# One visit fewer to the 64-column tiling: kv of two batches and two remainder tiles together, and the last q loaded early

## The chip, the cores and the metric

The kernel runs on one core of one Trainium2 chip. The metric is the device time of one execution in microseconds. Ratios are the mean time of one kernel's fast runs over the mean of the other's fast runs of the same rounds, so they are not quite the ratios of the medians that stand beside them.

## The reference, cut to what matters

```python
kv  = einsum('bhsd,bhse->bhde', k, v)              # 8 batches, 8 heads, 576 rows, head size 64
out = einsum('bhsd,bhde->bhse', q, kv)
x   = out / sqrt(mean(out*out, -1) + 1e-6) * g_norm  # then heads side by side: (8, 576, 512)
xn  = (x - mean) / sqrt(var + 1e-6) * g_ln
y   = x + relu(xn @ w_ch1) @ w_ch2                 # 512 -> 2048 -> 512
```

The two products of the last line are nearly all of the TensorE work. A batch has 576 rows, which is four tiles of 128 and a remainder of 64. The remainders of two batches share one tile ("remainder tile 5" holds those of batches 4 and 5, "remainder tile 7" those of 6 and 7), and the four remainder tiles make up a ninth block at the end.

## The kernel before

Everything is written as one stream per engine, in an order that an agenda of slots sets by hand. A slot is four 128x512 matmuls; block b has 32 slots from 32b, 16 for the first product and 16 for the second. What an agenda entry emits stands in each engine's queue at that place. It fixes the order, not the time.

```python
def kv_of(*bs):                      # k^T v per head: 64-column matmuls, then four casts for two batches
    kv_ps = ps_m.tile([128, len(bs), HP, D], f32, tag="misc", name="kv_ps")
    for i, b in enumerate(bs):
        ...                          # 40 matmuls per batch
    for i, b in enumerate(bs):
        kvp = held[b] = kv_pack[b % 4]
        nc.scalar.copy(kvp[:D, :, :D], kv_ps[:D, i])
        nc.scalar.copy(kvp[D:, :, D:], kv_ps[D:, i])

def turn_q_dma(b):                   # q copied to another order by VectorE, transposed by DMA
    ...
    nc.vector.tensor_copy(q_p.rearrange("p j h d -> p h j d"), q_in[b % NB])
    nc.sync.dma_start_transpose(...)

def rem_tile(b):                     # stationary of 64 columns: again the 64-column tiling
    mms = []
    for half, bb in enumerate((b - 1, b)):
        qt, kp = qts.pop(bb), held.pop(bb)
        mms.append((slice(half * 64, (half + 1) * 64), lambda hp, qt=qt: qt[:, J, hp, :64], kp))
    ...

# plan_tile(s, make, turn_at, on_pe, x_at): matmuls and square and reduce at slot s; root,
# reciprocal, y, x, xc at x_at (s + 2 if not given); the deviation 4 later; the transpose at turn_at

at(132, lambda: load_batches((("q", 6), ("k", 6), ("v", 6), ("k", 7), ("v", 7)), turned_q(5)))
at(164, lambda: load_batches((("q", 7),), turned_q(6)))
for s, bs, rem, x_at, tn in (..., (152, (6, 7), 5, 154, 160)):
    at(s, lambda bs=bs: kv_of(*bs))
    plan_tile(s + .1, lambda rem=rem: rem_tile(rem), tn, False, x_at)
plan_tile(210, lambda: rem_tile(7), 216, False)
```

So kv of batches 6 and 7, with remainder tile 5, is one visit to the array's 64-column tiling in the second product of block 4, and remainder tile 7 is another in the second product of block 6.

## Time and profile before

| | before |
|---|---|
| median of the first three runs | 288.96 us (288.9 to 289.06) |
| TensorE busy, share of the span | 97% |
| longest wait of TensorE after 20 us | none worth naming |
| starts of consecutive 128x512 matmuls | 0.216 us apart |

TensorE is the bound (97% busy, and 91% of the chain that ended last): what counts is the sum of its matmuls and anything that makes its queue stand. I cut the stretch of the change at the first matmul of each product, which the timeline gives. Below is the view of busy time by stretch: block 4's second product, block 5's first, block 5's second with block 6's first, and block 6's second. The columns are the stretch, its length, then busy time and instructions of TensorE, its weight loads, VectorE, ScalarE and GpSimd, the granted clock, the DMA share and the GB/s.

```profile
154.71:170.46 15.75, 15.64 (x155) 7.90 (x156) 9.55 (x21) 5.68 (x15) 1.53 (x3) 1.00 0.99 144
170.46:184.95 14.49, 14.38 (x78) 6.95 (x78) 9.83 (x22) 12.54 (x27) 0.00 (x0) 1.00 0.48 96
184.95:213.47 28.52, 28.36 (x143) 13.43 (x145) 16.27 (x35) 15.03 (x34) 0.00 (x0) 1.00 0.39 79
213.47:227.73 14.26, 14.21 (x71) 6.43 (x72) 8.60 (x19) 4.11 (x11) 0.00 (x0) 1.00 0.37 79
```

A product alone is 64 x 0.216 = 13.8 us. The first row has 1.9 us more, which is the visit of kv and remainder 5 and tile 0 of batch 6; the last has 0.44 more, which is the visit of remainder 7: 0.22 for its eight matmuls and 0.22 for entering and leaving the 64-column tiling, of which entering is 0.09 (214.98 to 215.29, where 0.216 is usual). Note in the second row that ScalarE (the fourth busy time) works 12.5 us of 14.5: the first product is where ScalarE has least room. Together the four stretches take 73.02 us.

### The profile page before, as it was taken

The numbers are of one execution on the slowest core, as the hardware profiler recorded it, in microseconds if no ns is written. First come the engines' busy times: TensorE is split into PE (matmuls) and PEld (weight loads), VectorE is DVE, ScalarE is ACT, GpSimd is POOL, SyncE is SP. The second block draws the span as 40 slices with busy tenths as digits, with TensorE's granted clock in tenths as the row PEclk, the third lists the DMA queues.
The fourth block names the chain that finished last, engine by engine and source line by source line (L and its number), as shares of the span: only waits on it lengthen the run. The fifth ranks groups of instructions, "written<-read, shape, count | busy, mean of one in ns | idle before, by whom it ended". The sixth has DMA issues, their size and how long they took to land.

```text
span 286.7 us, 5727 instructions
## 1 busy us (share of the span) xinstructions
PE 277.8 (97%) x2269; PEld 158.0 (55%) x2295; DVE 150.0 (52%) x331; ACT 152.9 (53%) x333; POOL 43.1 (15%) x73
## 2 busy tenths in 40 slices
PE   7889999999999999999999999999999999999995
PEld 3579755995579654454444544444444444444444
DVE  5774119937997883774376475763679200220022
ACT  3477844995468643971387338911893066016500
POOL 8522510041036005000710020000000000000000
PEclk9999999999999999999999999999999999999999
DMA  7999999969997979986999995047203410230033
GB/s 215 198 209 202 201 191 197 214 111 188 144 180 124 185 141 172 214 101 127 159 215 190 120 160 135 18 82 158 56 18 72 95 37 0 48 81 19 0 73 76
DMA packets 67419, 36.76 MB, mean 128 GB/s; under 512 B 35517, under 2 KB 62525, under 8 KB 67393
## 3 DMA queue, kind: packets, MB, share of 16 engines
q0 software_dynamic: 28720, 18.29, 44.2%
q1 hardware_dynamic: 38160, 17.39, 30.4%
q10 hardware_dynamic: 512, 0.72, 0.8%
q8 instruction: 18, 0.29, 0.5%
q14 instruction: 9, 0.07, 0.1%
HBM read 36.71 MB, written 9.44 MB: 161 GB/s over the span
## 4 chain that ended last, share of the span: by engine, by line
PE 91%; DMA 2%; DVE 2%; ACT 2%; issue 1%; DVEq 0%; POOLq 0%
PE p L432 43%; PE p L416 42%; PE o_ps L274 3%; DMA v_in<-in_v_dram 2%; PE kv_ps L247 2%; ACT m L419 1%; DVE x_blk L292 0%; DVE xc L552 0%; ACT xT_blk L353 0%; PE tp L351 0%; ACT rms L311 0%; PE odd L226 0%; DVE ss L518 0%; PE tp L559 0%; DVE ss L301 0%
## 5 line engine op out<-in xcount | busy, mean ns | idle before, releaser
L416 PE MATMUL p<-xT_blk,w_sb 128*128 128x128 bf16 (+2 forms) x1015 | 131.2, 285 | 0.9
L432 PE MATMUL p<-w_sb,m 128*128 128x512 bf16 (+2 forms) x592 | 126.2, 368 | 1.2 <-issue 0.5
L419 ACT ACTIVATE m<-p 128x512 bf16<-128x512 f32 x144 | 85.2, 596 | 46.7 <-PE p L416 44.3
L416 PEld LDWEIGHTS <-w_sb 128*128 128x128 bf16 x1024 | 78.6, 98 | 44.5 <-issue 1.1
L432 PEld LDWEIGHTS <-m 128*128 128x128 bf16 x608 | 57.3, 98 | 62.9
L437 DVE SCALAR_TENSOR_TENSOR o_sb<-p,rstd,x_blk 128x512 f32<-128x512 f32 (+2 forms) x38 | 27.2, 721 | 47.7 <-PE p L432 42.1
L280 ACT ACTIVATE sq<-o_ps 128x512 f32<-128x512 f32 x35 | 20.9, 596 | 26.7 <-PE o_ps L274 26.5
L343 ACT ACTIVATE dev<-x_blk,st_blk 128x512 f32<-128x512 f32 x36 | 25.7, 714 | 13.1 <-DVE st_blk L329 13.1
L301 DVE TENSOR_REDUCE ss<-sq 128x8 f32<-128x512 f32 x35 | 23.7, 678 | 17.0 <-ACT sq L280 17.0
L335 DVE SCALAR_TENSOR_TENSOR xc<-x_blk,st_blk,g_ln_sb 128x512 bf16<-128x512 f32 x34 | 25.6, 752 | 1.2
L306 DVE TENSOR_TENSOR y<-o_ps,inv 128x512 f32<-128x512 f32 x33 | 22.8, 692 | 3.1
L325 DVE SCALAR_TENSOR_TENSOR x_blk<-y,g_norm_sb 128x512 f32<-128x512 f32 x33 | 22.8, 692 | 1.1
L318 DVE RECIPROCAL inv<-rms 128x8 f32<-128x8 f32 x36 | 7.3, 202 | 23.3 <-ACT rms L311 23.3
L425 DVE RECIPROCAL rstd<-rstd 128x4 f32<-128x4 f32 x9 | 1.6, 175 | 29.9 <-ACT rstd L424 29.8
L311 ACT ACTIVATE rms<-ss,eps_sb 128x8 f32<-128x8 f32 x36 | 10.6, 295 | 11.5 <-DVE ss L301 11.3
L274 PEld LDWEIGHTS <-qt 128*128 128x128 bf16 (+1 forms) x156 | 10.3, 100 | 6.0 <-issue 0.4
L274 PE MATMUL o_ps<-kv_pack,qt 128*128 128x128 bf16 (+1 forms) x156 | 13.6, 220 | 0.0
L98 POOL COPY gate<-qt 1x1 bf16<-1x1 bf16 x5 | 0.9, 177 | 82.4 <-DMA qt<-q_p 82.4
L199 PE MATMUL p<-fill_sb 128*128 128x512 bf16 x26 | 7.8, 452 | 1.3 <-DVE eps_sb L138 1.2
L252 ACT CAST kv_pack<-kv_ps 64x256 bf16<-64x256 f32 x7 | 2.6, 366 | 10.7 <-PE kv_ps L247 10.7
L343 ACT ACTIVATION_READ_ACCUMULATOR dev<-x_blk,st_blk 128x1 f32 x36 | 6.8, 190 | 0.0
L247 PEld LDWEIGHTS <-k_in 128*64 128x64 bf16 x280 | 4.9, 112 | 2.4 <-issue 2.3
(82 smaller groups left out, 112.6 us busy)
## 6 DMA issues: line engine op xcount, KB each, us to landing
out_dram<-o_sb SPq DMA_DIRECT2D x66, 128.0 KB, 2.6
w_sb<-in_moe_w_ch_dram POOLq DMA_DIRECT2D x8, 512.0 KB, 15.2
q_in<-in_q_dram POOLq DMA_DIRECT2D x7, 320.0 KB, 9.7
k_in<-in_k_dram POOLq DMA_DIRECT2D x7, 320.0 KB, 8.7
v_in<-in_v_dram POOLq DMA_DIRECT2D x7, 320.0 KB, 10.3
q_in<-in_q_dram POOLq DMA_DIRECT2D x8, 256.0 KB, 10.5
k_in<-in_k_dram POOLq DMA_DIRECT2D x7, 256.0 KB, 9.3
v_in<-in_v_dram POOLq DMA_DIRECT2D x7, 256.0 KB, 12.3
```

Of the source, the lines that this page charges most:

```text
L247: nc.tensor.matmul(kv_ps[hh * D:hh * D + D, i, hp, :], lhsT=k_in[b % NB][:, h, j, :], rhs=v_in[b % NB][:, h, j, :], start=(j == 0), stop=( ...
L274: nc.tensor.matmul(flat[rows, hp * 128:(hp + 1) * 128], lhsT=lhsT_of(hp), rhs=kvp[:, hp, :], start=True, stop=True)
L280: nc.scalar.activation(self.sq_t, self.o_ps, func=AF.Square)
L301: nc.vector.tensor_reduce(self.ss, self.sq_t, axis=AX.X, op=ALU.add)
L306: nc.vector.tensor_mul(self.y_t, self.o_ps, self.inv().to_broadcast([128, H, D]))
L325: nc.vector.scalar_tensor_tensor(x_blk[:, ts].rearrange("p (h d) -> p h d", h=H), in0=self.y_t, scalar=1.0, in1=g_norm_sb.to_broadcast([12 ...
L335: nc.vector.scalar_tensor_tensor(self.xc_t, in0=x_blk[:, self.ts], scalar=st[:, 1, self.ts:self.ts + 1], in1=g_ln_sb, op0=ALU.add, op1=ALU ...
L343: nc.scalar.activation(dev, x_blk[:, ts], func=AF.Square, bias=st[:, 1, ts:ts + 1], accum_out=st[:, 2, ts:ts + 1])
L416: nc.tensor.matmul(p1[:, i, :], lhsT=w1_sb[:, kk, de * 128:(de + 1) * 128], rhs=blk[2][:, kk, sl], start=(kk == 0), stop=(kk == nK - 1))
L419: nc.scalar.activation(m1[:, de0:de0 + per, sl], p1, func=AF.Relu)
L432: nc.tensor.matmul(p2[:, c0:c1], lhsT=m1s[b][:, de, ts * 128:(ts + 1) * 128], rhs=w2_sb[:, de, c0:c1], start=(de == 0), stop=(de == nDe - 1))
L437: nc.vector.scalar_tensor_tensor(o_sb[:, c0:c1], in0=p2[:, c0:c1], scalar=rstds[b][:, ts:ts + 1], in1=blks[b][0][:, ts, c0:c1], op0=ALU.mu ...
```

## The change

Its intent: enter and leave the 64-column tiling once instead of twice. For that remainder 7 must stand beside kv of 6 and 7, so q of batch 7 is loaded and turned (transposed) beside that of 6, the visit moves nine slots later with kv of 7 before that of 6, and the tiles of batch 6 move too.

```diff
-            qt, kp = qts.pop(bb), held.pop(bb)
+            qt, kp = qts[bb], held[bb]
+            if b < B - 1:
+                del qts[bb], held[bb]
...
-    at(132, lambda: load_batches((("q", 6), ("k", 6), ("v", 6), ("k", 7), ("v", 7)),
+    at(132, lambda: load_batches((("q", 6), ("q", 7), ("k", 6), ("v", 6), ("k", 7), ("v", 7)),
                                  turned_q(5)))
-    at(164, lambda: load_batches((("q", 7),), turned_q(6)))
...
-                                 (152, (6, 7), 5, 154, 160)):
+                                 (161, (7, 6), 5, 162, 168)):
...
-    plan_tile(210, lambda: rem_tile(7), 216, False)
+    plan_tile(161.2, lambda: rem_tile(7), 170, False, 164)
...
-                                *((b, 32 * b - 43.3, 32 * b - 32, 5) for b in range(5, B))):
+                                (5, 116.7, 128, 5), (6, 147, 165, 4.5), (7, 151, 192, 5)):
```

## The prediction

> **What bounds the kernel now.** I read the page first: busy shares, then the chain that ended last.
>
> ```profile
> PE 277.8 (97%) x2269; PEld 158.0 (55%) x2295; DVE 150.0 (52%) x331; ACT 152.9 (53%) x333; POOL 43.1 (15%) x73
> ...
> PEclk9999999999999999999999999999999999999999
> ...
> PE 91%; DMA 2%; DVE 2%; ACT 2%; issue 1%; DVEq 0%; POOLq 0%
> ```
>
> The end is set by TensorE's own queue, at full clock. The view of TensorE's waits, asked over the whole span, has no wait after the first 20 us worth a microsecond:
>
> ```profile
> PE even L226 <- DMA v_in<-in_v_dram: 1.4, 1, 1.4
> PE p L199 <- DVE eps_sb L138: 1.2, 1, 1.2
> PE p L432 <- issue: 0.5, 3, 0.2
> PE tp L559 <- DVE xc L552: 0.4, 1, 0.4
> ```
>
> From 60 us on TensorE runs matmul after matmul; the starts of 128x512 matmuls lie 0.216 us apart (three starts in a row just before the late remainder visit: 214.55, 214.76, 214.98). So the program is a sum of matmuls, and a change counts only if it removes TensorE time or makes TensorE wait. A slot of the agenda is four such matmuls, 4 x 0.216 = 0.864 us; a block has 32 slots, 16 for its first product (L416) and 16 for its second (L432).
>
> The timeline of TensorE and of ScalarE around the visits that move shows both sides of this change (columns: start us, us, engine, line, operation, tiles, count, idle before and releaser):
>
> ```profile
> 161.71 1.46 PE L247 MATMUL kv_ps<-v_in,k_in 128*64 128x64 bf16 x80
> 163.00 0.39 PE L274 MATMUL o_ps<-kv_pack,qt 128*64 128x128 bf16 x8
> 163.32 7.08 PE L432 MATMUL p<-w_sb,m 128*128 128x512 bf16 x31
> 170.24 0.39 PE L274 MATMUL o_ps<-kv_pack,qt 128*128 128x128 bf16 x4
> ```
>
> ```profile
> 163.21 0.37 ACT L252 CAST kv_pack<-kv_ps 64x256 bf16<-64x256 f32 x1 [3.95 <-PE kv_ps L247]
> 163.58 0.37 ACT L253 CAST kv_pack<-kv_ps 64x256 bf16<-64x256 f32 x1
> 163.97 0.37 ACT L252 CAST kv_pack<-kv_ps 64x256 bf16<-64x256 f32 x1
> 164.35 0.37 ACT L253 CAST kv_pack<-kv_ps 64x256 bf16<-64x256 f32 x1
> 164.75 0.60 ACT L280 ACTIVATE sq<-o_ps 128x512 f32<-128x512 f32 x1
> ```
>
> Here kv of 6 and 7 (80 small matmuls) is followed at once by remainder tile 5 (8 matmuls), whose kv was cast long ago; the four casts of the fresh kv run while TensorE is back at large matmuls. The late visit, remainder 7 alone, stands in the middle of block 6's second product:
>
> ```profile
> 214.55 0.81 PE L432 MATMUL p<-w_sb,m 128*128 128x512 bf16 x3
> 215.29 0.41 PE L274 MATMUL o_ps<-kv_pack,qt 128*64 128x128 bf16 x8
> 215.63 1.04 PE L432 MATMUL p<-w_sb,m 128*128 128x512 bf16 x4
> ```
>
> [...]the last large matmul before the late visit started at 214.98, the first tile matmul at 215.29, 0.309 us later where the usual distance is 0.216, so entering costs 0.09. [...]in this trace the one 1.38 us wait of TensorE (before 8.20 us) left the granted clock at full. [...]both batches' kv share one 128x512 f32 tile, and here the first cast started at 163.21, after all 80 kv matmuls had been issued (the eight after them started at 163.00).
>
> **The change part by part.**
>
> 1. *One visit fewer.* The late visit: from the large matmul at 214.98 to the next at 215.63 is 0.656 us, less the 0.216 that one large matmul takes anyway: 0.44. Its four pairs in steady run are 0.052 to 0.056 apart, about 0.22 us, and those are still paid in the merged visit. Saved: 0.44 - 0.22 = **0.22 us**. The visit of kv and remainder 5 moves from block 4's second product (slot 152) to slot 161, block 5's first product; its own cost (161.40 to 163.32, less 0.216: 1.71 us) is the same in either place.
>
> 2. *A new wait for the casts.* In the built order of the changed kernel the eight matmuls of remainder 7 come straight after the eight of remainder 5, and the first waits for ScalarE: it reads kv of 6 and 7, which the 80 matmuls just before have made. Order (7, 6) puts 6's casts last, and the first matmul reads 6's. On the distances of the old trace: kv starts at t; remainder 5 at t+1.29; remainder 7 could start at t+1.51; first cast at t+1.50, fourth ends at t+3.01 (161.71 to 164.72), plus 0.05 for the signal: t+3.06. TensorE idles about **1.55 us**. [...]
>
> 3. *ScalarE and VectorE in block 5's first product.* The old trace of this stretch, 170.4 to 184.3:
>
> ```profile
> 170.40:184.30 13.90, 13.79 (x77) 6.71 (x75) 9.27 (x20) 11.88 (x26) 0.00 (x0) 1.00 0.50 101
> ```
>
> ScalarE (fourth pair of numbers) is busy 11.88 of 13.90, because each slot needs one 0.60 us relu. The change puts in four casts (1.5), two squares (1.2), two roots (0.6) and two deviations (1.8): about 5 us, and takes out about 0.9 (tile 3 of batch 6 moves to slot 178). 11.9 + 5.1 - 0.9 = 16.1 against 13.9 + 1.55 of stall + the visit of 1.7 = 17.2: it fits, barely. VectorE gets the two remainder tiles at 0.69 (reduce) + 2.6 (reciprocal, y, x, xc) = 3.3 us each, ahead of tile 0 of batch 6, in order. I walked the three queues by hand with the trace's durations, from slot 160 at 168.7 (170.4 less the 1.71 now still to come): casts end 172.66; relu of slot 161 at 173.96; VectorE finishes remainder 5's xc at 177.4 and 7's at 180.0; only then tile (6,0)'s reduce, 180.04 to 180.73. ScalarE stands at that tile's root until 180.76, with the relu of slot 167 behind it. TensorE has three buffers for this product, so slot 170 must wait for that relu: 181.60 in place of 181.28 (0.32), then 0.33 and 0.12 in the next two slots, after which it runs level. Sum **0.77 us**, the least certain term: a lag 0.7 us less erases it, 0.7 more doubles it.
>
> 4. *Loads and turns.* Two loads less late, none less in all; one 1x1 gate copy drops. Batch 7's q takes its 3.5 us of traffic ahead of k and v, so the last v lands near 163 instead of 159.60. kv now starts near 169.6: hidden. q of 7 turned: VectorE copies it near 160.6 to 161.4, SyncE issues its transpose behind that of batch 5's last tile, near 165.6, and with the 5.9 us of batch 6's (161.05 to 166.91) it lands near 171.5, just before the casts end at 172.66. Hidden by 1.2 us. Batch 5's last transposed tile landed at 167.35; its product now starts at 168.7 instead of 170.4. Hidden by about 1.3.
>
> Sum: 288.96 - 0.22 + 1.55 + 0.77 = 291.06. I shade the third term a little and say **290.8**.
>
> **The rivals.** (a) *The saving alone*: the 0.22 us shows, 288.7. It needs the casts to be done when remainder 7 starts; the old trace says they end 1.5 us after that[...]. Against it. (b) *Only the cast wait*, with the third term absorbed: 288.96 - 0.22 + 1.55 = 290.3. For it: TensorE's own stall gives ScalarE 1.5 us to catch up. (c) *A transfer becomes the wait*: more traffic up to 163 us beside the transposes of q could delay batch 5's last transposed tile past 168.7, or q of 7 past 172.7. A microsecond or two late means 291.5 to 292.5. Against: both margins are over 1 us and the loads end well before. (d) *ScalarE becomes the bound of the whole first product*: 16.1 against 17.2 us says no, but if remainder tiles lag, more than three slots stall: 292. (e) The clock drops after the idle time: 1.55 us is close to the harmless 1.38 seen, so no.
>
> **Range and chances.** Range 289.7 to 292.0: below (b) by 0.6 if the casts start sooner than I think, above the sum by 0.9 if (c) or (d) joins in. Two per cent is 5.8 us either way. Faster by that is impossible from a visit worth 0.44 us in all; slower needs over twice the stall that I find. Chances: faster 0.01, same 0.97, slower 0.02.
>
> **What the new profile would show.** Step 1: no 128*64 matmuls in block 6's second product; one run of 80 and 16 in block 5's first. Step 2: a wait of remainder 7's first matmul for the kv casts of about 1.5 us, the largest late wait in TensorE's view. Step 3: small waits of the L416-line matmuls for relus near 181 to 184, the root of tile (6,0) waiting for its reduce. Step 4: no wait for a transfer. I am wrong if the first idle is near zero (the wait asks for less than the last cast), if the turned q and not a cast ends it, or if the loss is spread over many slots.

That no other matmul runs while one waits, on which step 2 rests, was the assumption; the changed kernel's trace shows it. The 3.5 us of traffic in step 4 is the estimate: the two loads of a q move 320 and 256 KB (the page), which at the 186 GB/s of the trace before from 140 to 164 us takes 3.2 us. Measured, the last v landed 4.5 us later (164.11 for 159.60).

## The result, and the profile after

The changed kernel took 291.81 us in the median of four runs (291.51 to 292.11), the kernel before 288.93 in the same rounds: ratio 1.0102, 95% interval 1.0085 to 1.0120. It is about 1% slower. The profiled runs lie 292.11 against 288.75, so the two traces differ by 3.4 us, somewhat more than the medians' 2.9: the profiled run of the changed kernel is the slowest of its four.

The view of TensorE's waits over the whole span of the changed kernel, the three rows of it that are new (what waited, for what; us in total, times, longest):

```profile
PE o_ps L274 <- ACT kv_pack L253: 1.4, 1, 1.4
...
PE o_ps L274 <- DMA qt<-q_p: 0.9, 1, 0.9
...
PE p L418 <- ACT m L421: 0.5, 2, 0.3
```

The rows left out are those of the start and of the issue, as before. Remainder 7 (L274) waits for a cast, then for a transpose of q, and the first product (L418) waits twice for relus. The same three on TensorE's timeline:

```profile
169.56 1.46 PE L247 MATMUL kv_ps<-v_in,k_in 128*64 128x64 bf16 x80
170.85 0.39 PE L274 MATMUL o_ps<-kv_pack,qt 128*64 128x128 bf16 x8
172.61 0.22 PE L274 MATMUL o_ps<-kv_pack,qt 128*64 128x128 bf16 x1 [1.37 <-ACT kv_pack L253]
173.71 0.41 PE L274 MATMUL o_ps<-kv_pack,qt 128*64 128x128 bf16 x7 [0.88 <-DMA qt<-q_p]
...
182.73 1.02 PE L418 MATMUL p<-xT_blk,w_sb 128*128 128x512 bf16 x4 [0.29 <-ACT m L421]
183.92 2.86 PE L418 MATMUL p<-xT_blk,w_sb 128*128 128x512 bf16 x11 [0.16 <-ACT m L421]
```

The eight matmuls of remainder 5 go through at once. The first of remainder 7 (batch 6's half) starts when the last cast is done, at 172.61; the second (batch 7's half) needs q of 7, which is not turned until 173.7. From 170.85 to 174.28 no matmul of the first product runs, though its last transposed tile had landed at 168.28: what stands behind a waiting matmul here waited with it. Around 182 to 184 the product stands twice more. The timeline of VectorE and of ScalarE says why; the rows are remainder 7's xc, the reduce of tile (6,0) behind it, and the root that waits for that reduce with a relu behind it:

```profile
180.51 0.75 DVE L335 SCALAR_TENSOR_TENSOR xc<-x_blk,st_blk,g_ln_sb 128x512 bf16<-128x512 f32 x1
181.18 0.68 DVE L301 TENSOR_REDUCE ss<-sq 128x8 f32<-128x512 f32 x1
```

```profile
181.90 0.30 ACT L311 ACTIVATE rms<-ss,eps_sb 128x8 f32<-128x8 f32 x1 [1.31 <-DVE ss L301]
182.10 0.58 ACT L421 ACTIVATE m<-p 128x512 bf16<-128x512 f32 x1
```

Busy time by stretch, cut at the same four products:

```profile
154.79:168.60 13.81, 13.76 (x64) 6.23 (x64) 7.17 (x14) 2.50 (x7) 0.00 (x0) 1.00 1.21 184
168.60:188.56 19.96, 17.05 (x171) 8.66 (x172) 12.83 (x29) 14.96 (x35) 0.00 (x0) 1.00 0.45 92
188.56:217.31 28.75, 28.59 (x147) 13.63 (x149) 18.48 (x41) 16.63 (x38) 0.00 (x0) 1.00 0.28 60
217.31:231.12 13.81, 13.76 (x64) 6.27 (x64) 5.69 (x12) 2.50 (x7) 0.00 (x0) 1.00 0.36 77
```

The four stretches take 76.33 us, 3.31 more than before. The last row shows what the change was made for: 13.81 in place of 14.26, so the late visit's 0.45 us is gone. The second row shows the price: in 19.96 us TensorE is busy 17.05. Outside these stretches the two traces run alike: 0.08 us of difference before them, at 154.7, and the rest of the end's 3.4 us lies within.

### The profile page after: what moved, and what is told of

Same layout as the page of the kernel before. It is cut to its first block, busy times and chain, and to the rows that moved or that the text cites. A ratio compares the mean times of both kernels' runs of the same rounds, so it can differ in the third digit from the quotient of the medians.

```text
span 290.1 us, 5726 instructions
## 1 busy us (share of the span) xinstructions
PE 279.2 (96%) x2270; PEld 158.3 (55%) x2295; DVE 149.6 (52%) x331; ACT 152.1 (52%) x333; POOL 42.9 (15%) x72
## 4 chain that ended last, share of the span: by engine, by line
PE 86%; DVE 5%; DMA 4%; ACT 3%; issue 1%; SPq 0%; DVEq 0%
PE p L434 42%; PE p L418 39%; PE o_ps L274 2%; DMA qt<-q_p 2%; DMA gn_row<-in_g_norm_dram 2%; PE kv_ps L247 1%; ACT m L421 1%; DVE xc L335 1%; DVE x_blk L325 0%; DVE x_blk L292 0%; DVE y L306 0%; DVE xc L554 0%; DVE ss L301 0%; ACT xT_blk L353 0%; ACT rms L311 0%
## 5 line engine op out<-in xcount | busy, mean ns | idle before, releaser
L418 PE MATMUL p<-xT_blk,w_sb 128*128 128x128 bf16 (+2 forms) x1015 | 131.8, 285 | 1.4 <-ACT m L421 0.5
L418 PEld LDWEIGHTS <-w_sb 128*128 128x128 bf16 x1024 | 78.5, 98 | 45.5 <-issue 2.4
L274 PE MATMUL o_ps<-kv_pack,qt 128*128 128x128 bf16 (+1 forms) x156 | 13.8, 220 | 2.2 <-ACT kv_pack L253 1.4
L274 PEld LDWEIGHTS <-qt 128*128 128x128 bf16 (+1 forms) x156 | 10.4, 100 | 8.1 <-DMA qt<-q_p 2.6
L199 PE MATMUL p<-fill_sb 128*128 128x512 bf16 x26 | 8.6, 489 | 1.3 <-DVE eps_sb L138 1.2
```

Source lines behind the costliest of these rows:

```text
L274: nc.tensor.matmul(flat[rows, hp * 128:(hp + 1) * 128], lhsT=lhsT_of(hp), rhs=kvp[:, hp, :], start=True, stop=True)
L418: nc.tensor.matmul(p1[:, i, :], lhsT=w1_sb[:, kk, de * 128:(de + 1) * 128], rhs=blk[2][:, kk, sl], start=(kk == 0), stop=(kk == nK - 1))
```

## The experiments

My theory A: the loss is remainder 7 standing at the head of TensorE's in-order queue for what it reads, and its later work on VectorE and ScalarE crowding block 5's first product. Rival R: the kv visit moved into the first product and q of 7 ahead in the loads cost the time, whatever remainder 7 does. Rival S: the two waits at remainder 7 add up. Eleven kernels ran. Labels follow the order in which I made them; the ninth was not run.

### Remainder 7 back in its own visit

```diff
-    plan_tile(161.2, lambda: rem_tile(7), 170, False, 164)
+    plan_tile(210, lambda: rem_tile(7), 216, False)
```

> The changed kernel with remainder tile 7 put back to its own late visit; loads, turns, kv of 7 and 6 and remainder 5 stay as changed. Theory A (the loss is remainder 7 standing in TensorE's queue: first for the casts of kv, then for the turned q of batch 7, then its work on VectorE and ScalarE crowds block 5's first product): the waits go, the saving of 0.22 us goes too; within 0.5 us of the kernel before, 288.9 to 289.4. Rival R (the visit of kv moved into the first product, and q of batch 7 loaded ahead of k and v, cost the time whatever remainder 7 does): 291 to 292.

Measured: 288.62 us, before 289.30 in the same rounds, ratio 0.9987 (0.9967 to 1.0006). In the trace the four stretches take 73.02 us, as before. Rival R falls: loads, early turn, order of kv and the moved visit cost nothing by themselves. Block 5's first product takes 16.20 us here (168.56 to 184.76), and that is the yardstick below: the changed kernel's 19.96 is 3.76 more, of which 0.22 is remainder 7's own matmuls and 3.54 is loss.

### One wait at a time

In these three, remainder 7 reads the turned q of batches 4 and 5, or their kv, or both, which have been there for long. Their outputs are wrong, which doesn't matter for the times. The instructions and their number stay. OLD_Q and OLD_KV stand for the True or False of each run; lines that only keep the old tiles alive are left out.

```diff
-            qt, kp = qts[bb], held[bb]
+            qb = bb - 2 if b == B - 1 and OLD_Q else bb
+            kb = bb - 2 if b == B - 1 and OLD_KV else bb
+            qt, kp = qts[qb], held[kb]
...
```

Old q, fresh kv:

> The changed kernel, but remainder tile 7 reads the turned q of batches 4 and 5, long there (wrong result on purpose); the kv that it reads is fresh. Takes the wait for the turned q away and leaves that for the casts. Theory A: TensorE's idle at remainder 7 falls from about 2.7 to about 1.5 us, so the time falls by 0.7 to 1.2 us against the changed kernel, to 290.6 to 291.1. Rival R: no change, 291.8.

Measured: 291.00 us, before 289.30, ratio 1.0063 (1.0046 to 1.0080). TensorE's largest wait is the cast alone, and the first product takes 18.88 us (168.82 to 187.70): 18.88 - 16.20 - 0.22 = 2.46 lost. The visit, from the first kv matmul to the next large one, takes 3.40 us (169.77 to 173.17) against 1.61 without remainder 7; less 0.22 that leaves 1.57 for the wait, and 0.89 for the crowding.

Old kv, fresh q:

> The changed kernel, but remainder tile 7 reads the kv of batches 4 and 5, long cast (wrong result on purpose); the turned q is fresh. Takes the wait for the casts away and leaves that for the turned q. Theory A, with the two waits running side by side (the later one counts): TensorE still idles until q of 7 is turned, so under 0.4 us is won, 291.4 to 291.9. Rival S (the two waits add up): 1.4 us is won, about 290.4.

Measured: 291.51 us, ratio 1.0088 (1.0066 to 1.0110). The wait for the turned q is now 1.8 us in one piece, ending 4.50 us after the head of the product (169.51 to 174.01; in the changed kernel 5.11, 168.60 to 173.71). The visit takes 3.88 us (170.47 to 174.35), 2.05 lost. With the cast wait away the first product took some 0.6 us less (19.37 for 19.96), where that wait's own length is 1.4. Even this 0.6 is not the cast's: batch 6's transpose of q took 3.79 us to issue here and 4.44 in the changed kernel's trace, so q of 7 went out that much sooner. The two waits run side by side, and rival S falls. The gains of single removals therefore do not sum to the gain of both.

Both old:

> The changed kernel, but remainder tile 7 reads both q and kv of batches 4 and 5 (wrong result on purpose). No wait at remainder 7 is left; its work on VectorE and ScalarE stays in block 5's first product. Theory A: the 2.7 us idle goes, the crowding stays at 0.9 or grows (to 1.5 us) as the other two engines no longer catch up in TensorE's idle time; with 0.22 saved, 289.6 to 290.3. Rival (crowding is only an echo of the idle time): 288.7.

Measured: 291.08 us, ratio 1.0070 (1.0048 to 1.0092). This is a miss. No wait at remainder 7 is left (TensorE's waits show none on a cast or a turned q), and still 0.7% of loss stays. Two things had taken its place. ScalarE's stand at tile (6,0)'s root grew from 1.31 to 1.83 us, and TensorE's longest wait for a relu from 0.29 to 0.81:

```profile
180.78 0.30 ACT L311 ACTIVATE rms<-ss,eps_sb 128x8 f32<-128x8 f32 x1 [1.83 <-DVE ss L301]
```

```profile
PE p L423 <- ACT m L426: 1.0, 2, 0.8
PE p L423 <- DMA xT_blk<-xc: 0.5, 1, 0.5
```

The first product takes 18.43 us (169.02 to 187.45), so 18.43 - 16.20 - 0.22 = 2.01 us are lost to crowding, where the changed kernel loses 0.9. VectorE has the same work for the two remainder tiles (3.3 us each in the changed kernel's trace), and the 2.7 us in which TensorE idled had been time for it to catch up. ScalarE had used that time too: 0.6 of the 2.0 us falls right behind the visit (171.82 to 175.88 for sixteen matmuls of 3.46), where casts and squares now hold up its first relu until 173.98 and tile (6,0) waits 0.22 us for remainder 5's y. The second row is batch 5's last transposed tile, which came late by 0.5 us at the head of the product, before the 18.43 us begin. So the expectation's 1.5 us for the crowding was too small, and I had not counted on the last tile.

### The crowding by itself

Remainder 7's y, x, xc and deviation are put off to the end of the first product, its result held in a PSUM tile that is free until then.

```diff
+        pool = (ps2, "p2") if b == B - 1 else ()
-        return Tile(mms, blks["rem"], b // 2)
+        return Tile(mms, blks["rem"], b // 2, *pool)
...
-    plan_tile(161.2, lambda: rem_tile(7), 170, False, 164)
+    plan_tile(161.2, lambda: rem_tile(7), 188, False, 175.8)
```

> The changed kernel, with remainder 7's y, x, xc and deviation put off to the end of block 5's first product (its result held in a PSUM tile that the second product does not need yet). Both waits stay, 2.7 us; what is tested is the crowding. Theory A: VectorE reaches tile (6,0)'s reduce 2.6 us sooner, ScalarE no longer stands at its root, the three short waits for relus go: 0.6 to 0.9 us won, 290.9 to 291.2. Rival (ScalarE's sheer load makes them): under 0.3 us won.

Measured: 291.13 us, before 288.96, ratio 1.0086 (1.0062 to 1.0111). The interval overlaps that of the changed kernel, so the times alone decide little; the trace does. After the visit the first product runs level, 13.63 us to its end (173.82 to 187.45), exactly as with remainder 7 in its own visit (171.13 to 184.76), and no wait for a relu is left in TensorE's view. The crowding comes from VectorE's order: remainder 7's chain ahead of tile (6,0)'s reduce. (The deviation put off with it is ScalarE's work, but in the changed kernel it ran at 182.58, after ScalarE's stand of 1.31 us for that reduce, so it did not make the first and longest of the waits.) Block 5's second product takes 0.36 us more in return (14.62 against 14.26): the put-off chain delays the eviction that frees a PSUM tile (TensorE waits 0.2 us for o_sb in its view).

With both waits and the crowding taken away (old q and old kv, chain late):

> Remainder 7 in the merged visit reads q and kv of batches 4 and 5 (wrong result on purpose: no wait), and its y, x, xc and deviation are put off to the end of block 5's first product. Takes both terms of the loss away at once. Theory A (the loss is TensorE's idle at remainder 7 plus the crowding of VectorE and ScalarE behind it, and where one goes the other grows): block 5's first product runs level; within 0.2 per cent of the kernel before, 288.8 to 289.5 (0.22 saved, up to 0.4 given back in the second product, where the put-off work delays an eviction; the last transposed tile of batch 5 may still be late by up to 0.6). Rival (something else in the merged visit costs): 290.5 or more.

Measured: 289.12 us, before 288.72, ratio 1.0014 (1.0001 to 1.0026). The four stretches take 73.36 us, 0.34 over the kernel before. The known terms give the same: 0.36 in the second product, 0.21 left at the first (16.63 - 16.20 - 0.22; it falls right behind the visit, in the sixteen matmuls from 171.32 to 175.00), less 0.22 saved, which is 0.35. Nothing else is hidden in the merged visit.

### The saving by itself

The kernel before, with remainder 7 beside remainder 5 at slot 152, reading old q and old kv.

```diff
...
-    plan_tile(210, lambda: rem_tile(7), 216, False)
+    plan_tile(152.2, lambda: rem_tile(7), 162, False, 156)
```

> The kernel before, with remainder tile 7 moved beside remainder 5 into the visit in block 4's second product, reading the q and kv of batches 4 and 5 (wrong result on purpose), so that nothing waits. Measures the saving of one visit by itself. Theory A: 0.22 us, 288.7 to 288.8 where the kernel before has 288.95, ratio 0.9992; the interval may touch 1. Rival (a visit costs more than its two entries in the trace[...]): 288.4 or less.

Measured: 289.01 us, before 288.96, ratio 1.0006 (0.9993 to 1.0019), where 0.9992 had been expected. The trace shows the saving and where it went: block 6's second product falls to 13.82 us, the visit grows from 1.61 to 1.84 (so 0.21 is saved), and block 5's first product takes 14.82 in place of 14.49, where its relus now meet remainder 7's chain (TensorE waits 0.17 us for one). Net 0.11 us more. Even where nothing waits and the visit lies in a second product, the neighbours take the 0.2 us back.

### Trying to repair the wait for q

Transpose of batch 7's q from ScalarE's queue, idle at that time:

```diff
-        nc.sync.dma_start_transpose(
+        (nc.scalar if b == 7 else nc.sync).dma_start_transpose(
```

> The changed kernel, with the transpose of q of batch 7 issued by ScalarE's queue, which is idle then, in place of SyncE's, where it stood behind batch 6's and behind the last tile of batch 5. Right result. Theory A: it is issued near 161.5 instead of 167.2 and lands before the casts end at 172.6, so TensorE idles about 1.5 us and not 2.7; time as where remainder 7 reads old q, 290.5 to 291.1. Rival ([...]the last tile of batch 5 is then late): no gain, and a wait at the head of block 5's first product.

Measured: 298.00 us, before 288.96, ratio 1.0322 (1.0296 to 1.0348): a bad idea, and what the rival foretold came (no gain, a wait at the head of the product). The built program makes transposes of two queues wait for each other: ScalarE, which had done nothing since 159.3, issued its transpose at 166.13, just after batch 6's had landed at 165.96, and batch 5's last tile on SyncE was issued at 171.62, after that one had landed at 171.56. The head of the first product waited 5.4 us, and the granted clock was 0.69 over 170 to 174 us and 0.50 over 174 to 178. No run lets the two go at once, so what that would do was not shown.

The same, with the upper halves of the casts on VectorE:

```diff
-            nc.scalar.copy(kvp[D:, :, D:], kv_ps[D:, i])
+            (nc.vector.tensor_copy if len(bs) == 2 else nc.scalar.copy)(
+                kvp[D:, :, D:], kv_ps[D:, i])
```

> As the run before, and of the four casts two (the upper halves) are done by VectorE, idle there, beside ScalarE's two. Right result. Theory A: the casts end 0.75 us after they start in place of 1.5, TensorE idles about 0.75 us; 289.9 to 290.4. If the two engines do not run side by side on that one PSUM tile, no gain over the run before.

Measured: 298.36 us, ratio 1.0335 (1.0316 to 1.0353). The transposes spoil the time as above. The casts did not run side by side either: ScalarE's at 177.86 and 178.72, VectorE's at 178.26 and 179.12, each waiting for the other engine's before it. All four read one PSUM tile; in the last experiment, with tiles apart, the two engines' casts do run together (166.67 and 166.70; VectorE's are released there by kv's matmuls and not by a cast of ScalarE's).

q of 6 and 7 turned ten slots sooner, on SyncE as before:

```diff
-                                (5, 116.7, 128, 5), (6, 147, 165, 4.5), (7, 151, 192, 5)):
+                                (5, 116.7, 128, 5), (6, 137, 165, 4.5), (7, 142, 192, 5)):
```

> The changed kernel with q of 6 and 7 copied and transposed some ten slots sooner, ahead of batch 5's last tiles. Right result. Theory A: the wait for the turned q of 7 and any lateness of batch 5's last tile go; the wait for the casts (1.4 to 1.6 us) and the crowding (0.9 us) stay: 290.6 to 291.3, as where remainder 7 read old q. Rival (traffic still holds the transposes up): 291.5 or more, with a wait for a turned q.

Measured: 297.21 us, before 288.72, ratio 1.0285 (1.0248 to 1.0321). A miss again, in the direction of the rival but by another path. SyncE's timeline of this run (start us, us of issuing):

```profile
151.67 7.46 SPq L206 DMA_TRANSPOSE qt<-q_p  x1
159.18 1.89 SPq L355 DMA_TRANSPOSE xT_blk<-xc  x1
161.18 5.34 SPq L206 DMA_TRANSPOSE qt<-q_p  x1
166.56 1.26 SPq L355 DMA_TRANSPOSE xT_blk<-xc  x1
```

For the changed kernel the same two transposes of q, after most of the loads:

```profile
160.02 4.44 SPq L206 DMA_TRANSPOSE qt<-q_p  x1
...
167.19 3.08 SPq L206 DMA_TRANSPOSE qt<-q_p  x1
```

A transpose of q issued in the thick of the loads took 7.46 us to issue and 14.2 to land, where one issued after them took 3.1 to issue. Behind two such, in one queue, batch 5's tiles came late, and the head of the first product waited 4.5 us. That wait has an echo: from 174 to 178 us the granted clock was 0.57 here, and 0.50 in the run with the 5.4 us wait, where the changed kernel's two shorter waits (1.37 and 0.88 us) left it at 1.00.

### A version meant to beat both

Early turns, the visit at slot 156 in block 4's second product, kv in four PSUM tiles so that casts overlap.

```diff
+    def kv_apart(*bs):   # as kv_of, but even and odd heads of each batch in a PSUM tile of their own
+        ...
+            nc.scalar.copy(kvp[:D, :, :D], ts[b, 0][:D])
+            nc.vector.tensor_copy(kvp[D:, :, D:], ts[b, 1][D:])
...
-                                 (161, (7, 6), 5, 162, 168)):
+                                 (156, (7, 6), 5, 158, 163.5)):
...
-    plan_tile(161.2, lambda: rem_tile(7), 170, False, 164)
+    plan_tile(156.2, lambda: rem_tile(7), 166, False, 160)
...
-                                (5, 116.7, 128, 5), (6, 147, 165, 4.5), (7, 151, 192, 5)):
+                                (5, 116.7, 128, 5), (6, 137, 163, 4.6), (7, 142, 192, 5)):
```

> A right version of the change's aim: early turns as above; the merged visit in block 4's second product (slot 156), where VectorE and ScalarE have room; kv of 7 and 6 in four PSUM tiles (even and odd heads of each), so that 7's casts run during 6's matmuls, and ScalarE and VectorE cast side by side. Theory A: TensorE idles about 0.45 us at remainder 7 (signal 0.21, cast 0.43, signal 0.05, less remainder 5's 0.22), crowding 0 to 0.4 us, saving 0.22: 289.0 to 289.6, better than the changed kernel by over 2 us and no better than the kernel before. Rival: beats the kernel before by more than 0.2 us.

Its signals and cast are from traces: 0.21 us from remainder 5's first matmul to the first cast (170.85 to 171.06 in the changed kernel), 0.05 from the last cast's end to remainder 7 (172.56 to 172.61), 0.43 for a cast on VectorE (the run with split casts).

Measured: 293.98 us, before 288.72, ratio 1.0183 (1.0168 to 1.0198), a miss. It carries the early turns' fault. TensorE's timeline:

```profile
165.83 1.46 PE L268 MATMUL kv_ps<-v_in,k_in 128*64 128x64 bf16 x80 [0.49 <-DMA v_in<-in_v_dram]
167.10 0.42 PE L296 MATMUL o_ps<-kv_pack,qt 128*64 128x128 bf16 x8
167.91 0.22 PE L296 MATMUL o_ps<-kv_pack,qt 128*64 128x128 bf16 x1 [0.40 <-DVE kv_pack L274]
170.45 0.41 PE L296 MATMUL o_ps<-kv_pack,qt 128*64 128x128 bf16 x7 [2.32 <-DMA qt<-q_p]
```

One part worked as expected: with PSUM tiles apart the wait for the casts is 0.40 us (1.37 in the changed kernel). The rest did not: v arrives 0.5 us late, and q of 7 another 2.3. The clock adds to it: it was 0.994 over the span, which of 292.0 us is 1.75 us of full clock lost, and the sixteen large matmuls behind the visit took 5.15 us (170.79 to 175.94) where 3.46 is usual, so about 1.7 us of this run's loss is the lower clock. The longest wait before it was 2.32 us, with one of 0.40 shortly before. The 1.8 us wait with old kv left the clock at 1.00 (the sixteen matmuls behind it took 3.47 us); what else differs between these runs and sets the clock, no run separates. No run shows a right version of the merged visit that beats the kernel before. The saving is 0.22 us at most, the best cast wait measured is 0.40, so there is no room for one unless other 64-column work fills that wait.

## Why the prediction was right, and where its terms were off

The range of 289.7 to 292.0 round the predicted 290.8 held 291.81, and "within 2%" held. It held narrowly: the median lies 0.2 us below the range's upper end, which had been set for one of rivals (c) or (d) to join in, and one of the four runs (292.11) lies outside. Step by step, in trace time:

| step | predicted | measured | from |
|---|---|---|---|
| one visit less | -0.22 | -0.23 | last stretch 14.26 to 13.81, less 0.22 of matmuls paid again |
| wait for the casts | 1.55 | 1.57 | run with old q |
| turned q of 7 | hidden by 1.2 | 1.1 more than the casts | 3.54 lost in the changed kernel, 2.46 with old q |
| crowding of block 5's first product | 0.77 | 0.89 | run with old q; none with the chain late |
| batch 5's last tile | hidden by 1.3 | hidden by 0.3 | landed 168.28, product from 168.60 |
| sum | 2.1 | 3.3 in the trace, 2.9 in the medians | |

*Step 1 was right*, also in saying that nothing larger can be won. *Step 2 was right* in mechanism and size. *Step 3 was right in size*, and the named place (the root of tile (6,0), behind remainder 7's xc on VectorE) is where it was found. Slot by slot it said 0.32, 0.33 and 0.12 us; with old q the trace has 0.46, 0.33 and 0.11. ScalarE was busy 14.96 us of the product's 19.96, so rival (d) did not come true. What step 3 did not see is that this term depends on the other: without TensorE's idle time it is 2.0 us, not 0.9.

*The term that failed is in step 4*: "it lands near 171.5, just before the casts end at 172.66. Hidden by 1.2 us." I took the old trace's 3.2 us to issue and 5.9 to land for a transpose of q. But in the change batch 6's transpose is issued at 160.02, while the loads, longer by q of 7, still run until 164.11 (last v landed; step 4 had said near 163). It took 4.44 us to issue; the queue behind it moved by 1.6 us, batch 7's went out at 167.19 instead of 165.6, and TensorE could go on at 173.71, 6.5 us after that and not 5.9. That put 1.1 us on the wait and ate 1.0 of the 1.3 us of slack of batch 5's last tile. One of the prediction's own signs of being wrong thus came true at the second half of remainder 7: the turned q, and not a cast, ended its wait. Rival (c) of the prediction named this cause and gave it 291.5 to 292.5, which is where the time fell; I weighed it too low because I looked at when loads end and not at what the transposes meet on their way.

The size of this term varies from run to run. In the nine traces that load and turn q of 6 as the changed kernel does, that transpose took 3.75 to 4.44 us to issue, and the changed kernel's own is the longest; q of 7 came 0.5 us after the time of the casts with old kv, 0.8 with the chain late, 1.1 in the changed kernel. So the 3.3 us of this trace may overstate the usual loss, as the medians' 2.9 suggest.

That loads slow the transposes is shown as a pattern only: the same transpose takes 3.1 us to issue after the loads, 4.4 at their end and 7.5 in their midst. What holds it up, no run separates.

## What to carry to other kernels

When a consumer is moved next to its producer in an in-order queue to save a switch, count what the queue then waits for: here 0.22 us of switching was bought with 2.7 us of standing. Waits at one place can run side by side (here 1.6 and 2.1 us alone, 2.7 together), so remove them one at a time and together before adding up gains, and expect crowding on the other engines to grow when the idle time that hid it goes (0.9 to 2.0 us here). Before a DMA is moved earlier or later, look at what traffic it will meet (3.1 us to issue a transpose of q after the loads, 7.5 among them) and what stands behind it in its queue, not only at whether its data is there.
